# Weight splits three blocks ahead with four buffers; one pair for a slot's transposed rows, one buffer for the next stage's blocks

## The chip, the cores and the metric

The kernel runs on one core of a Trainium2 chip. Times are device microseconds (us) of one execution. The engines that matter are TensorE (PE for matmuls and transposes, PEld for loading its stationary operand), VectorE (DVE), ScalarE (ACT), GpSimd (POOL, which computes and also issues the indirect DMAs) and SyncE (SP, which issues the plain DMAs). Each engine works through its own queue in order.

## The reference

The kernel computes three layers on 1792 rows of 768 features, all in fp32:

```python
scores = scale * q @ k.T - log(S)
attn_out = sigmoid(scores) @ v                  # 4 x 12 heads, S = 448, 64 features
x = attn_out as [1792, 768]
expert_idx = argmax(x @ w_gate); gate_w = softmax(x @ w_gate)[expert_idx]
x = gate_w * (relu(x @ w1[expert_idx]) @ w2[expert_idx])      # 8 experts, 768 -> 1024 -> 768
g = x @ w2_gate;  out = (silu(g) * (x @ w2_val)) @ w2_out     # 768 -> 1536 -> 768
```

## The kernel before

Four stages follow one another: attention with the choice of experts, the expert stage, and two stages for the last layer, here called the first and the second GEMM.

The expert stage handles the 1792 rows in blocks of up to 128 rows of one expert, called slots. Slots 0 to 13 are the main ones, done one after the other; five half-filled ones (numbered from `NFX` = 17) run as background work between them. A matmul of fp32 quality is made of three with fp32r operands, so each weight block is split into a high part `whi` (a cast on ACT, line 811) and a low part `wlo` (a subtraction on DVE, line 813; for the first two blocks of w1 the last 256 columns are subtracted on POOL, line 815). `split_w` does that into the pool `wh`, which has `LA + 1` buffers for each part, and then has SP load the block of the next slot, if its expert differs (lines 817 to 820). `product` multiplies one block: six matmuls.

`seq` (line 844) is the list of blocks in their order: entries 0 to 3 are (1, 0, 4) to (1, 0, 7), the second half of w2 for slot 0; entries 4 to 9 are (0, 1, 0) to (0, 1, 5), w1 for slot 1; entries 10 to 15 are (0, 2, 0) to (0, 2, 5), w1 for slot 2; then w2 for slot 1, w1 for slot 3 and so on, 14 entries for each slot. The loop at line 1049 takes entry after entry: first `split_w` of the entry `LA` ahead, then all functions registered for this entry with `when`, in the order in which they were registered, then `product`. The whole is written inside `tc.manual_schedule()`: every engine issues its instructions in the order in which the program emits them. Across engines the framework inserts waits: an instruction that writes a tile waits until all uses of the tile that had the buffer before are over, wherever in the program these uses stand.

What is registered around the change:

- `gather(s)` (line 760): POOL issues an indirect DMA that fetches the rows of slot s into a tile `xg`. There are two buffers of `xg`. Slots 1 and 2 are gathered before entry 0; slot 3 by `early_x` of slot 1; the first background slot at entry 5.
- `early_x` (line 856) for slots 1 and 2: `transposes` puts the rows on PE through PSUM tiles `pt` (two buffers, shared by all transposes) into `xh` and `xl` (ACT casts, DVE subtracts). For slot 1 that is at entry 0, for slot 2 at entry 3. For later slots `tx` transposes at (1, s-2, 1) and evacuates at (1, s-2, 3).
- `bg_x`, `bg_h` (lines 926 and 961): six or four transposes of a background slot, at an entry whose kind and block number stand in `FREE`. For the first background slot `bg_x` comes at entry 10.
- `load_item` and `prep_next` (lines 668 and 892): load a block of the last layer's gate and value weights into a tile `w` (`WB` buffers) and split it into `wgh` and `wgl` (four buffers each). The first four are prepared during the expert stage, the others during the first GEMM (lines 1140, 1141 and 1150).

In the first GEMM, `gemm1(f, ci)` does 36 matmuls on up to 512 columns; its two halves use the gate block and the value block of f.

Of the kernel before, what the change touches and what calls it, by code (L numbers as in the profile page):

```python
# [22 lines left out]
def sigmoid_attention_moe_swiglu_kernel(  # L23
# [23 lines left out]
    KD = DM // P  # L47
# [26 lines left out]
    def split(hi, lo, src, eng=None):  # L74
        if eng is nc.vector:
            nc.vector.tensor_copy(hi, src)
        else:
            nc.scalar.copy(hi, src)  # L78
        nc.vector.tensor_sub(lo, src, hi.bitcast(F32))  # L79
# [60 lines left out]
    def load_w(kind, j, e, cond=None):  # L140
        src = (w1, w2)[kind][bass.ds(e, 1), j * P:(j + 1) * P, :].rearrange("o p f -> p (o f)")
        if cond is None:
            nc.sync.dma_start(raws[kind][j], src)
        else:
            nc.sync.dma_start(raws[kind][j], src, cond=cond)
# [500 lines left out]
            V.tensor_scalar(pos2, pos[:, hs_], 1, None, op0=ALU.logical_shift_left)  # L646
            V.tensor_tensor(pos2, pos2, upper.to_broadcast([P, NH0]), op=ALU.bitwise_or)

    LA = 2
    ectx = ExitStack()  # L650
    early = ectx.enter_context(tc.tile_pool(name="early", bufs=2, side="right", reuse_waits="tile"))
    ps_t = ctx.enter_context(tc.tile_pool(name="pst", bufs=2, space=PS, reuse_waits="tile"))
# [2 lines left out]
    mctx = ExitStack()  # L655
    wh = mctx.enter_context(tc.tile_pool(name="wh", bufs=LA + 1, reuse_waits="tile"))
    xp = mctx.enter_context(tc.tile_pool(name="xp", bufs=2, reuse_waits="tile"))
# [3 lines left out]
    KEEP = 2  # L661
    KS = K2 - KEEP

    WB = 2
    r64 = {}
    wsp = {}

    def load_item(key):
        kind, f = key
        r64[key] = early.tile([P, DM], F32, tag="w", name="w", bufs=WB)  # L670
        nc.sync.dma_start(r64[key], wgd["gv".index(kind) * K2 + f])

    def prep(key):
        hi = early.tile([P, DM], F32R, tag="wgh", name="wgh", bufs=4)
        lo = early.tile([P, DM], F32R, tag="wgl", name="wgl", bufs=4)
        split(hi, lo, r64.pop(key))
        wsp[key] = (hi, lo)
# [75 lines left out]
    xg = {}  # L753
    act = {}
# [5 lines left out]
    def gather(s):  # L760
        xg[s] = xp.tile([P, DM], F32, tag="xg", name="xg", bufs=2)
        nc.gpsimd.indirect_dma_start(
            out=xg[s][:, :], out_offset=None, in_=xd[:, :],
            in_offset=bass.IndirectOffsetOnAxis(ap=perm_g[:, s:s + 1], axis=0))

    def transposes(src, m, tag, bufs):
        hi = xp.tile([P, m * P], F32R, tag=tag + "h", name=tag + "h", bufs=bufs)
        lo = xp.tile([P, m * P], F32R, tag=tag + "l", name=tag + "l", bufs=bufs)
        pts = []
        for j0 in range(0, m, 4):  # L770
            mm = min(4, m - j0)
            pt = ps_t.tile([P, 512], F32, tag="tr", name="pt")
            for j in range(mm):
                nc.tensor.transpose(pt[:, j * P:(j + 1) * P],
                                    src[:, (j0 + j) * P:(j0 + j + 1) * P], ident)
            pts.append((pt, slice(j0 * P, (j0 + mm) * P), mm * P))

        def evac():
            for pt, sl, mm in pts:
                split(hi[:, sl], lo[:, sl], pt[:, :mm])  # L780
        return (hi, lo), evac

    def relu(s):
        hsb[s] = hsp.tile([P, FF], F32, tag="hs", name="hsb", bufs=1)
        nc.scalar.activation(hsb[s].rearrange("p (m f) -> p m f", m=2), hps.pop(s), AF.Relu)
# [3 lines left out]
    def yout(s):  # L789
        ysbs[s] = xp.tile([P, 2, HW + 1], F32, tag="ysb", name="ysb", bufs=1)  # L790
        nc.scalar.activation(ysbs[s][:, :, :HW], yps.pop(s)[:, :, :HW], AF.Copy,
                             scale=gsl[:, s:s + 1])

    def ystore_rows(s):
        ysb = ysbs.pop(s)
        nc.gpsimd.tensor_copy(ysb[:, :, HW:].bitcast(I32),
                              perm_g[:, None, s:s + 1].to_broadcast([P, 2, 1]))
        nc.gpsimd.indirect_dma_start(
            out=yd.rearrange("n h c -> n (h c)"),
            out_offset=bass.IndirectOffsetOnAxis(ap=pos[:, s:s + 1], axis=0),  # L800
            in_=ysb.rearrange("p h c -> p (h c)"), in_offset=None)
# [4 lines left out]
    def split_w(kind, s, j):  # L806
        w = (FF, DM)[kind]
        hi = wh.tile([P, FF], F32R, tag="hi", name="whi")
        lo = wh.tile([P, FF], F32R, tag="lo", name="wlo")
        r = raws[kind][j]  # L810
        nc.scalar.copy(hi[:, :w], r)  # L811
        w0 = w - PSH.get((kind, j), 0)
        nc.vector.tensor_sub(lo[:, :w0], r[:, :w0], hi[:, :w0].bitcast(F32))  # L813
        if w0 < w:
            nc.gpsimd.tensor_sub(lo[:, w0:w], r[:, w0:w], hi[:, w0:w].bitcast(F32))  # L815
        ws[kind, s, j] = (hi, lo)
        if s + 1 < NS0:
            if (s + 1) not in ev:
                load_ev(s + 1)
            load_w(kind, j, ev[s + 1], cond=nv[s + 1])  # L820
# [18 lines left out]
    EJ = 5  # L839
    YD, GJ = 3, 4  # L840
    PJ = (6, 4)
    XJ = (4, 7)
    NJ = 4
    seq = [(1, 0, j) for j in range(NJ, KF)] + [(0, 1, j) for j in range(KD)]
    for s in range(2, NS0 + 1):
# [6 lines left out]
    def when(kind, s, j, f):  # L852
        at.setdefault((kind, s, j), []).append(f)

    for s in (1, 2):
        def early_x(s=s):
            act[s], e = transposes(xg.pop(s), KD, "x", 2)
            e()
            if s == 1:
                gather(3)  # L860

        when(1, 0, XJ[s - 1], early_x)
    when(0, 1, 1, lambda: yout(0))
    when(0, 1, 2, lambda: ystore_rows(0))
    for s in range(1, NS0):
        e = {}

        def tx(s=s, e=e):
            act[s], e["x"] = transposes(xg.pop(s), KD, "x", 2)

        def th(s=s, e=e):
            hact[s], e["h"] = transposes(hsb.pop(s), KF, "h", 1)

        if s >= 3:
            when(1, s - 2, 1, tx)
            when(1, s - 2, 3, lambda e=e: e["x"]())
        if s == 1:
            when(0, 2, 1, lambda: relu(1))
        else:
            when(1, s - 1, 1, lambda s=s: relu(s))  # L880
        if s < L:
            when(0, s + 1, 3, th)
            when(0, s + 1, 4, lambda e=e: e["h"]())
        if s < L:
            when(*((0, s + 2, 1) if s + 2 <= L else (1, L, 0)), lambda s=s: yout(s))
            when(1, s + 1, YD, lambda s=s: ystore_rows(s))
        if s >= 4:
            when(1, s - 3, GJ, lambda s=s: gather(s))

    items = [(kind, f) for f in range(K2) for kind in "gv"]  # L890

    def prep_next(key):
        prep(key)
        i = items.index(key) + WB
        if i < len(items):
            load_item(items[i])

    pre = [lambda i=i: load_item(items[i]) for i in range(WB)]
    pre += [lambda key=key: prep_next(key) for key in items[:4]]
    for i, f in enumerate(pre):  # L900
        when(1, 3 + i, PJ[i % 2], f)
    R0 = E
    when(0, R0 + 2, 0, lambda: (make_yT(0), load_y(0)))
    for j in range(KD):
# [95 lines left out]
    def extra():  # L1000
        for s in [*range(NS0, NFX), *range(NFX + NH0, NS)]:
            ev[s] = nc.values_load(slot_e[0:1, s:s + 1], engines=[SP], min_val=0, max_val=E - 1,
                                   skip_runtime_bounds_check_because=why)
            sq = [(kind, s, j) for kind, m in ((0, KD), (1, KF)) for j in range(m)]
            for kind, _, j in sq:
                load_w(kind, j, ev[s])
            gather(s)
            act[s], e = transposes(xg.pop(s), KD, "x", 2)
            e()
            for key in sq[:LA]:  # L1010
                split_w(*key)
            for i, key in enumerate(sq):
                if i + LA < len(sq):
                    split_w(*sq[i + LA])
                if key == (1, s, 0):
                    relu(s)
                    hact[s], e = transposes(hsb.pop(s), KF, "h", 1)
                    e()
                product(*key)
            yout(s)  # L1020
            ystore_rows(s)

    hbp = post = ymid = None
    with tc.manual_schedule():
# [16 lines left out]
        yps[0] = ps_a.tile([P, 2, 512], F32, tag="a", name="yps")  # L1041
        for idx in range(LA):
            split_w(*seq[idx])
# [5 lines left out]
        for idx, key in enumerate(seq):  # L1049
            if idx + LA < len(seq):  # L1050
                split_w(*seq[idx + LA])
# [17 lines left out]
        with tc.If(nsl > NS0):  # L1069
            extra()  # L1070
# [68 lines left out]
        e = gemm1(0, 3)  # L1139
# [6 lines left out]
        for f in range(2, K2):  # L1146
            for ci in range(NC):
                e = gemm1(f, ci)
# [95 lines left out]
```

## Time and profile before

| | us |
|---|---|
| median of 3 runs | 1111.11 (1110.35 to 1111.57) |
| the profiled execution | 1114.54 |
| span of its instructions | 1112.7 |
| PE busy | 1071.4 (96% of the span) |
| DVE busy | 554.2 (50%) |
| ACT busy | 468.2 (42%) |
| POOL busy | 273.1 (25%) |

The span runs from the first to the last instruction of the profiled execution; 1.84 us of that execution lie around it. The expert stage takes from about 225 us to 581 us of the span, the first GEMM to about 928 us, the second to about 1097 us. "Granted clock" is TensorE's clock as a share of full speed (2.4 GHz); 0.5 is the lower level of 1.2 GHz.

In the timeline a row begins with its start and the time that it covers, both in us, then engine, line, operation, and output <- inputs; "xN" are N instructions of the kind in one row; brackets hold the idle time of the engine just before and what ended it. Matmuls overlap in the pipeline, so the distance between starts tells what one costs, not its length. In the windows view a row begins with the stretch and its length, then come the busy us (and instructions) of PE, PEld, DVE, ACT and POOL, the mean granted clock, the busy share of the DMA engines and GB/s.

### The profile page before, as it was taken

What the parts mean: (1) busy time and instruction counts of PE and PEld (TensorE: products, weight loads), DVE (VectorE), ACT (ScalarE), POOL (GpSimd) and SP (SyncE); (2) the same over time, 40 slices, a digit from 0 to 9 for tenths busy, and PEclk for the clock granted to TensorE, in tenths of its full rate; (3) what the DMA queues carried; (4) which work ended last, traced back from release to release, by engine and by line L of the source; (5) the groups of instructions that cost most, each with busy time, mean ns of one, the idle gap of its engine ahead of it and who ended that gap; (6) DMA issues with size and microseconds to landing.
All of it is one profiled execution on the core that took longest, in us unless ns stands there. A gap on an engine that the chain in (4) does not pass through costs nothing. (4 is left out here: it accounts for less than half of the span.)

```text
span 1112.7 us, 16190 instructions
## 1 busy us (share of the span) xinstructions
PE 1071.4 (96%) x5970; PEld 850.2 (76%) x5970; DVE 554.2 (50%) x851; ACT 468.2 (42%) x646; POOL 273.1 (25%) x234
## 2 busy tenths in 40 slices
PE   8999999899999999888989999999999999999996
PEld 5556555476767677766778888888888889999996
DVE  4686777676665677666643334444432225111110
ACT  6676766166566677566642211111111124112110
POOL 3656566341132222121110022222210000000101
PEclk9999999899999999999999999999999999999999
DMA  9999996845585776868441334444321134322220
GB/s 206 272 278 253 271 252 202 321 143 183 194 288 163 267 236 201 289 220 279 137 153 57 118 124 147 147 147 147 118 77 51 68 100 131 102 76 76 80 86 29
DMA packets 130533, 186.06 MB, mean 167 GB/s; under 512 B 51520, under 2 KB 95040, under 8 KB 130448
## 3 DMA queue, kind: packets, MB, share of 16 engines
q1 hardware_dynamic: 124400, 156.04, 45.3%
q0 software_dynamic: 6048, 28.92, 7.4%
q8 instruction: 49, 0.80, 0.3%
q14 instruction: 36, 0.29, 0.1%
HBM read 195.99 MB, written 40.85 MB: 213 GB/s over the span
## 5 line engine op out<-in xcount | busy, mean ns | idle before, releaser
L734 PE MATMUL psf<-y,wgh 128*128 128x512 f32 (+1 forms) x1152 | 321.0, 365 | 0.0
L813 DVE TENSOR_TENSOR wlo<-wraw,whi 128x768 fp32r<-128x768 f32 (+1 forms) x186 | 196.9, 1074 | 115.8 <-ACT whi L811 113.2
L734 PEld LDWEIGHTS psf<-y,wgh 128*128 128x128 f32 x1152 | 206.3, 189 | 32.8
L811 ACT CAST whi<-wraw 128x768 fp32r<-128x768 f32 (+1 forms) x186 | 170.3, 925 | 119.1 <-PE yps L835 59.9
L734 PE MATMUL psf<-y,wgl 128*128 128x512 f32 (+1 forms) x576 | 209.5, 364 | 0.0
L1185 PE MATMUL po<-y,hh 128*128 128x384 f32 x672 | 145.5, 334 | 0.6 <-ACT ob L1189 0.6
L739 ACT ACTIVATE sg<-psf 128x512 f32<-128x512 f32 (+1 forms) x48 | 26.1, 544 | 244.7 <-PE psf L734 244.7
L734 PEld LDWEIGHTS psf<-y,wgl 128*128 128x128 f32 x576 | 109.0, 189 | 17.2
L740 DVE TENSOR_TENSOR sg<-psf,sg 128x512 f32<-128x512 f32 (+1 forms) x48 | 30.0, 625 | 183.4 <-ACT sg L739 183.3
L1185 PEld LDWEIGHTS po<-y,hh 128*128 128x128 f32 x672 | 119.0, 188 | 0.9 <-ACT ob L1189 0.9
L236 ACT ACTIVATE a<-sc,logs 112x896 f32<-112x896 f32 x96 | 91.9, 1016 | 58.0 <-PE sc L234 58.0
L1185 PE MATMUL po<-y,hl 128*128 128x384 f32 x336 | 87.3, 334 | 0.0
L79 DVE TENSOR_TENSOR hl<-ht,hh 128x1280 fp32r<-128x1280 f32 x14 | 20.9, 1492 | 123.8 <-ACT hh L78 123.8
L1209 POOL DMA_INDIRECT out_dram<-ob,perm_c x13 | 13.0, 998 | 264.2 <-ACT ob L1208 264.2
L245 PE MATMUL pu<-a,vraw 112*64 112x448 f32 x384 | 77.5, 545 | 0.0
L173 POOL TENSOR_SCALAR w<-w 128x768 f32<-128x768 f32 x24 | 55.6, 2317 | 60.3 <-ACT w L162 60.2
L815 POOL TENSOR_TENSOR wlo<-wraw,whi 128x256 fp32r<-128x256 f32 x26 | 35.8, 1387 | 138.3 <-ACT whi L811 131.5
L78 ACT CAST hh<-ht 128x1280 fp32r<-128x1280 f32 x14 | 17.7, 1266 | 118.7 <-PE po L1185 118.7
L173 POOL TENSOR_SCALAR hl<-hl 128x768 f32<-128x768 f32 x12 | 27.5, 2292 | 138.1 <-ACT hl L162 138.1
L1185 PEld LDWEIGHTS po<-y,hl 128*128 128x128 f32 x336 | 60.9, 188 | 0.0
L835 PE MATMUL yps<-whi,hh 128*128 128x384 f32 x216 | 59.2, 355 | 0.0
L245 PEld LDWEIGHTS pu<-a,vraw 112*64 112x64 f32 x384 | 25.5, 136 | 40.9 <-issue 40.8
(235 smaller groups left out, 1600.7 us busy)
## 6 DMA issues: line engine op xcount, KB each, us to landing
wraw<-in_moe_w_dram SPq DMA_DIRECT2D x108, 384.0 KB
wraw<-in_moe_w_dram SPq DMA_DIRECT2D x78, 512.0 KB
ring<-in_moe_w_dram SPq DMA_DIRECT2D x30, 512.0 KB
ring<-in_moe_w_dram SPq DMA_DIRECT2D x40, 384.0 KB
r<-in_moe_w_gate_dram SPq DMA_DIRECT2D x12, 768.0 KB
wgd<-w POOLq DMA_DIRECT2D x24, 384.0 KB, 6.5
r<-in_moe_w_val_dram SPq DMA_DIRECT2D x12, 768.0 KB
w<-wgd SPq DMA_DIRECT2D x24, 384.0 KB
```

The costliest lines, as they stand in the source:

```text
L79: nc.vector.tensor_sub(lo, src, hi.bitcast(F32))
L173: nc.gpsimd.tensor_scalar(w, w, TINY, None, op0=ALU.is_ge)
L236: nc.scalar.activation(am[i][:, c], sc[:CP, :, :S], AF.Sigmoid, bias=logs[:CP], scale=SCALE)
L245: nc.tensor.matmul(pu[h * D:(h + 1) * D, :S], vt[:, h, c], a[:, c, h], start=(c == 0), stop=(c == C - 1))
L734: nc.tensor.matmul(ps[:, i, :cn], st[:, a], mv[:, j, :cn], start=(j == 0 and m == 0), stop=(j == KD - 1 and m == 2))
L739: nc.scalar.activation(sg[:, :cn], ps[:, 0, :cn], AF.Sigmoid)
L740: nc.vector.tensor_mul(sg[:, :cn], ps[:, 0, :cn], sg[:, :cn])
L811: nc.scalar.copy(hi[:, :w], r)
L813: nc.vector.tensor_sub(lo[:, :w0], r[:, :w0], hi[:, :w0].bitcast(F32))
L815: nc.gpsimd.tensor_sub(lo[:, w0:w], r[:, w0:w], hi[:, w0:w].bitcast(F32))
L835: nc.tensor.matmul(ps[:, m, :w], st[:, a], mv[:, m * w:(m + 1) * w], start=(j == 0 and i == 0), stop=(j == m_ - 1 and i == 2))
L1185: nc.tensor.matmul(po[:, m, :HW], st[:, f], wo[f][mv][:, m * HW:(m + 1) * HW], start=(f == 0 and x == 0), stop=(f == K2 - 1 and x == 2))
```

## The change

The weight split looks three entries ahead instead of two, and `wh` therefore has four buffers. The tiles `xh`, `xl` of a slot's transposed rows have one buffer each instead of two, and the tiles `w` of the last layer's blocks one instead of two. `early_x` of slot 2 moves from entry 3, (1, 0, 7), to entry 10, (0, 2, 0), where it is registered ahead of the first `bg_x`. The first `load_item` and the four early `prep_next` move by some entries; the second early `load_item` is gone, since `prep_next` loads the next block.

```diff
-    LA = 2
+    LA = 3
...
-    WB = 2
+    WB = 1
...
-    XJ = (4, 7)
...
     for s in (1, 2):
         def early_x(s=s):
-            act[s], e = transposes(xg.pop(s), KD, "x", 2)
+            act[s], e = transposes(xg.pop(s), KD, "x", 1)
             e()
             if s == 1:
                 gather(3)
 
-        when(1, 0, XJ[s - 1], early_x)
+        when(*((1, 0, 4) if s == 1 else (0, 2, 0)), early_x)
...
         def tx(s=s, e=e):
-            act[s], e["x"] = transposes(xg.pop(s), KD, "x", 2)
+            act[s], e["x"] = transposes(xg.pop(s), KD, "x", 1)
...
-    pre = [lambda i=i: load_item(items[i]) for i in range(WB)]
+    pre = [lambda: load_item(items[0])]
     pre += [lambda key=key: prep_next(key) for key in items[:4]]
     for i, f in enumerate(pre):
-        when(1, 3 + i, PJ[i % 2], f)
+        when(1, 4 + i, PJ[i % 2], f)
```

The same count of one buffer is put into `extra()`, which runs only when there are more slots than the 14 main and five background ones.

## Rows read from the trace of the kernel before

**Rows 1.** Busy time of each engine in the expert stage (windows view).

```profile
225.00:581.00 356.00, 334.18 (x1711) 253.62 (x1709) 236.69 (x272) 231.36 (x304) 84.07 (x88) 0.99 0.63 212
```

**Rows 2.** What PE waited for, 225 to 582 us: total, times, longest (waits).

```profile
PE pt L934 <- issue: 5.3, 3, 2.6
PE pt L964 <- DVE xl L79: 5.2, 2, 2.6
PE pt L964 <- DVE hl L79: 5.2, 2, 2.6
...
PE yps L835 <- DVE wlo L813: 0.7, 3, 0.2
```

**Rows 3.** The same view for PEld, the same stretch.

```profile
PEld yps L835 <- DVE wlo L813: 1.9, 4, 0.6
...
PEld hps L835 <- POOL wlo L815: 1.3, 4, 0.4
```

**Rows 4.** One background transpose that waits, all engines (timeline, 339 to 343 us).

```profile
339.58 0.83 ACT L811 CAST whi<-wraw 128x768 fp32r<-128x768 f32 x1 [0.21 <-PE yps L835]
340.32 0.85 ACT L78 CAST xh<-pt 128x512 fp32r<-128x512 f32 x2
341.32 1.01 DVE L79 TENSOR_TENSOR xl<-pt,xh 128x512 fp32r<-128x512 f32 x2
342.15 0.63 PE L964 MATMUL pt<-ident,bhs 128*128 128x128 f32 x4 [2.61 <-DVE xl L79]
```

**Rows 5.** A product that waits for its low part (timeline of PE, 265 to 267 us).

```profile
265.59 0.51 PE L835 MATMUL yps<-whi,hl 128*128 128x384 f32 x2
265.94 0.51 PE L835 MATMUL yps<-whi,hh 128*128 128x384 f32 x2
266.70 0.62 PE L835 MATMUL yps<-wlo,hh 128*128 128x384 f32 x2 [0.25 <-DVE wlo L813]
```

**Rows 6.** Transposes of slot 1 and of the first background slot (timeline of PE).

```profile
231.28 0.82 PE L774 MATMUL pt<-ident,xg 128*128 128x128 f32 x6
...
245.06 0.82 PE L934 MATMUL pt<-ident,xg 128*128 128x128 f32 x6
```

**Rows 7.** POOL in the same stretch: gathers of slots 3, 17 and 4 (timeline).

```profile
232.37 0.95 POOL L762 DMA_INDIRECT xg<-xd,perm_g  x1 [8.40 <-PE pt L774]
...
238.47 0.97 POOL L762 DMA_INDIRECT xg<-xd,perm_g  x1
...
243.68 2.92 POOL L815 TENSOR_TENSOR wlo<-wraw,whi 128x256 fp32r<-128x256 f32 x2 [1.59 <-ACT whi L811]
246.76 1.81 POOL L762 DMA_INDIRECT xg<-xd,perm_g  x1 [0.16 <-issue]
```

**Rows 8.** Issue to landing: gather at 232.37, at 246.76, all 16 after 225 us.

```profile
DMA to landing us min/median/max: 3.7/3.7/3.7
...
DMA to landing us min/median/max: 7.2/7.2/7.2
...
DMA to landing us min/median/max: 3.7/5.6/8.5
```

**Rows 9.** DMA traffic and granted clock in three stretches (windows view).

```profile
245.00:249.00 4.00, 4.00 (x22) 3.38 (x21) 2.92 (x3) 2.71 (x3) 3.41 (x3) 1.00 0.81 307
...
342.90:346.20 3.30, 3.30 (x14) 2.86 (x12) 0.96 (x1) 1.32 (x2) 0.00 (x0) 0.53 0.01 2
...
528.40:531.80 3.40, 3.37 (x21) 3.40 (x22) 1.00 (x2) 1.65 (x3) 0.00 (x0) 1.00 0.00 0
```

**Rows 10.** First GEMM: loads of `w` on SP, traffic after one, a value half (timeline, windows).

```profile
634.89 2.49 SPq L671 DMA_DIRECT2D w<-wgd  x2
...
643.55 0.62 PE L734 MATMUL psf<-y,wgh 128*128 128x512 f32 x2
...
650.77 8.48 SPq L671 DMA_DIRECT2D w<-wgd  x2
...
653.60:656.50 2.90, 2.90 (x15) 2.39 (x14) 0.00 (x0) 0.51 (x2) 0.00 (x0) 1.00 0.00 0
```

More of the change, by code (lines that the diff above doesn't have):

```diff
@@ L1007, in extra @@
             gather(s)
-            act[s], e = transposes(xg.pop(s), KD, "x", 2)
+            act[s], e = transposes(xg.pop(s), KD, "x", 1)
             e()
```

## The prediction

> **What bounds the kernel now.** I read the page's engine shares first, then the windows by stage, then the waits of PE and PEld in the stage that the change touches, then the timeline around each kind of wait. In the expert stage PE is busy 334.2 of 356.0 us, while DVE and ACT are busy about two thirds [rows 1]. So PE is the bound, and whatever holds it there goes into the total at full price: in the first GEMM PE has no idle time left that could absorb it (2.90 of 2.90 us in the stretch shown [rows 10]). What holds PE? Its named waits before transposes of background slots make up most of the list: 5.3, 5.2 and 5.2 us, at most 2.6 us each [rows 2]. Waits for a weight's low part are small: 0.7 us on PE in three places [rows 2], 1.9 and 1.3 us on PEld [rows 3], which partly cover the same time.
>
> **Three ahead with four buffers.** This can only remove waits for weight parts. The clearest place: pairs of matmuls of w2 start 0.35 us apart, and one pair starts 0.76 us after the pair before it, idle for `wlo` [rows 5]; that costs 0.41 us. Three such places are in the list [rows 2], so about 1.2 us; the shorter waits on PEld [rows 3] I put at about 0.6 us, since a wait of PEld is partly covered by the matmul that runs. One entry more of lead is worth three pairs of 0.35 us or more, about 1 us, against waits of at most 0.6 us [rows 3], so I take all of them as gone: -1.8 us. The bounds are 0 (what is late next is the same DVE queue) and -3.9 us (the three sums 0.7, 1.9 and 1.3 added as if none overlapped).
>
> The larger waits, those of the background transposes, stay. In the one shown, PE has finished a product, ACT casts a weight block, then the slot's rows, DVE subtracts, and only then is a PSUM tile free [rows 4]. The cast ahead of the rows was itself released by the product just finished. With three buffers, the split two ahead takes the buffer of the preceding entry; with four buffers, the split three ahead takes the buffer of that same entry. The chain keeps its length, 2.6 us.
>
> The split runs one entry earlier throughout, and the load behind it on SP with it, so a block still has 14 entries between its load and its split. One cast more ahead of entry 0 lies beside the fp32 products that run on PE until the transposes at 231.28 [rows 6]. Cost of both: nothing.
>
> **One pair for the transposed rows.** From slot 3 on, rows are evacuated at (1, s-2, 3), when the products of slot s-1 that read the single pair are three entries past. The writer finds it free; no wait. For slot 2 this isn't so at entry 3, and that is why its `early_x` has to stand behind entry 9.
>
> **Slot 2's rows at entry 10.** The step consists of six transposes on PE, two casts, two subtracts, and no DMA. Moved as work they cost what they cost now. But the step is moved past something on POOL's queue: the gather of the first background slot, emitted at entry 5. There are two `xg` buffers. At entry 5 one holds slot 3, the other slot 2, which is now read only at entry 10. So POOL's gather waits for PE's transposes at entry 10, and right behind these, at the same entry, stand the transposes of that very background slot, which need the gathered rows. PE works in order: it waits for a whole DMA that is under way today while PE works (issued at 238.47 [rows 7], used at 245.06 [rows 6]).
>
> How long? The place is 245.06 us. Slot 2's transposes no longer run at entry 3, so PE gets there about 0.6 us earlier and spends that again: they end near 245.3. A gather released by transposes starts about 0.3 us after their end (231.28 + 0.82, then 232.37 [rows 6, 7]), so at 245.6. It lands 3.7 to 8.5 us after issue, median 5.6 [rows 8]. Which? The gather at 246.76 is the nearest in place and takes 7.2 us [rows 7, 8]; the loads of the background weights are under way then, at 307 GB/s [rows 9], and they will be in the changed kernel too, as SP reaches them before the blocked work. I take 7.2: landing at 252.8, 7.7 us later than the background transposes start today. Bounds: 3.7 gives +4.2 us, 8.5 gives +9.0 us.
>
> A page says less: the Trainium skill, "DMA: Bandwidth & Descriptors", section "Anatomy of one DMA — SWDGE (gpsimd) path", fits such a transfer as 2.0 us plus its bytes at 436 GB/s, 2.9 us for 384 KB, an estimate of that page. By it this term would be +3.4 us; the trace disagrees, its fastest gather took 3.7 us [rows 8].
>
> Queued behind the waiting gather on POOL are a store of output rows (a short copy and an indirect DMA of about 1 us) and the low parts of (0, 2, 0) and (0, 2, 1), about 1.5 us each [rows 7]. The first is ready near 250, the second near 251.5, both before PE resumes at 252.8; if the gather lands at its fastest, the first is just in time. SP's loads for slot 3 wait for these two parts, some 6 us longer than now, and are wanted eleven entries later, over 15 us. ACT's evacuation of slot 2's rows ends within the wait. None of these adds to it.
>
> **The clock.** After one 2.6 us wait the clock that PE was granted had a mean of 0.53 over 3.30 us, which is the lower level of 1.2 GHz nearly throughout, and cost 3.30 x 0.47 = 1.5 us; after another of the same length, before 528.4, it stayed at 1.00 [rows 9]. A wait of 7.5 us will hardly go by without a fall, though part of the slow time may lie in the wait. I take +1.5 us, bounds 0 and +3.1 (two such stretches). The later 2.6 us waits will fall differently too; I count that as zero on the mean and up to two stretches either way.
>
> **One buffer for `w`.** The Trainium skill, "Trainium Kernel Development and Optimization", section "Best Practices", advises double buffers to overlap DMA with compute; by that rule the first GEMM would now wait for loads. In the trace, a load issued at 650.77 moves nothing more after 653.6, 2.8 us later [rows 10]. The tightest place is the pair prepared back to back: the second load would be issued at 634.89, land near 637.7, be split in about 1.8 us, and is first wanted at 643.55 [rows 10]: 4 us to spare. Elsewhere a whole `gemm1` lies between. Cost: nothing. The earlier `prep_next` of the expert stage are a slot or more apart, and SP's queue loses one early load.
>
> **Sum.** 7.7 + 1.5 - 1.8 = +7.4 us. The profiled execution took 1114.54 us with a span of 1112.7; it would be 1120.1 in span and about 1121.9. The median of the runs is 3.4 us below that execution, so 1111.1 + 7.4 = 1118.5 us.
>
> **Rivals.**
> A, the gather is not the last to arrive. If the rows are there in time (the framework finds a place for them after all), PE still waits at entry 10 for the PSUM tiles that slot 2's rows occupy: 2.6 us by the chain of rows 4. Then 2.6 - 1.8 = +0.8, 1111.9 us. Against it: two buffers can't hold three live tiles.
> B, faster: the extra buffer lets the cast in the chain of rows 4 run before PE's product ends. 0.83 us would fall out of each of the seven background waits [rows 2], 5.8 us; with the 1.8 that is 7.6. It decides only if the gather takes its shortest time and the clock holds: 4.2 - 7.6 = -3.4, 1107.7 us. Against it: the buffer arithmetic above.
> C, the lead doesn't do what it says: weight waits stay, since DVE's queue and not the buffer sets them. 7.7 + 1.5 = +9.2, 1120.3 us.
> D, the rule on double buffers holds in the first GEMM: `w` lands later than the 4 us to spare allow; with a load as slow as the slowest gather, 8.5 us instead of 2.8 [rows 8, 10], 1.7 us more, 1120.2 us.
>
> **How the numbers follow.** Forecast 0.72, A 0.11, B 0.04, C 0.10, D 0.03. The forecast's own bounds run from 4.2 - 3.9 = +0.3 to 9.0 + 3.1 = +12.1, with both ends unlikely as sums of extremes. A range from 1111.8 to 1122.3 takes in A, C and D and leaves out B and the high end. A measurement tells apart about 0.2% here, 2.2 us. Faster by more: B and a trace of luck with the clock, 0.05. Within 0.2% (1108.9 to 1113.3): A and the forecast's low end, 0.15. Slower: 0.80.
>
> **What would show it.** After: one new wait of PE of about 7 us before `bg_x`'s first transposes (near 245 us), ended by the gather; POOL idle until then, released by the transposes at line 774; weight waits on PE gone; the background waits still at 2.6 us; the first GEMM without idle time. The prediction is wrong if that gather is issued before slot 2's rows are transposed, or if the background waits shrink.

## The result, and the profile after

| | us |
|---|---|
| median of 5 runs after | 1120.31 (1118.38 to 1121.70) |
| median of 5 runs of before beside them | 1111.11 (1109.74 to 1113.92) |
| ratio after / before | 1.0078, 95% interval 1.0058 to 1.0099 |
| the profiled execution after, its span | 1118.38, 1116.5 |
| PE, DVE, ACT, POOL busy | 1070.0, 554.2, 467.6, 275.5 |

The changed kernel is 0.8% slower. PE does as much work as before (1071.4 us then); the difference is waiting and clock. From line 842 on, lines stand one earlier than before (934 is now 933, 964 is 963); the others kept their numbers.

What PE waited for in the expert stage of after, 225 to 586 us (waits view: engine, output, line, releaser, then total us, times, longest). It answers [rows 2].

```profile
PE pt L933 <- DMA xg<-xd,perm_g: 6.7, 1, 6.7
PE pt L933 <- issue: 5.3, 3, 2.6
PE pt L963 <- DVE xl L79: 5.2, 2, 2.6
PE pt L963 <- DVE hl L79: 5.2, 2, 2.6
```

One line is new, the wait for gathered rows. The three below it are the old ones to the tenth. They hold seven waits of background transposes, of which five take 2.6 us; the other two, both under "issue", take 1.2 and 1.5 us (at 314.6 and 376.8 us). No line for `wlo` is left, here or on PEld, where [rows 2, 3] had 0.7, 1.9 and 1.3 us.

The place of the new wait, PE of after (timeline; it answers the second row of [rows 6]):

```profile
250.23 1.51 PE L933 MATMUL pt<-ident,xg 128*128 128x128 f32 x6 [6.74 <-DMA xg<-xd,perm_g]
251.40 1.20 PE L835 MATMUL hps<-whi,xh 128*128 128x512 f32 x2
```

And POOL's queue in the same stretch of after (timeline; it answers [rows 7]), with the gather's landing below (view of line 762, 243 to 244.5 us; it answers [rows 8]):

```profile
232.69 2.92 POOL L815 TENSOR_TENSOR wlo<-wraw,whi 128x256 fp32r<-128x256 f32 x2 [1.00 <-ACT whi L811]
243.77 0.97 POOL L762 DMA_INDIRECT xg<-xd,perm_g  x1 [8.16 <-PE pt L774]
244.75 0.48 POOL L796 COPY ysb<-perm_g 128x2 int32<-128x2 int32 x1
245.52 1.00 POOL L798 DMA_INDIRECT yd<-ysb,pos  x1 [0.29 <-POOL ysb L796]
246.54 1.41 POOL L815 TENSOR_TENSOR wlo<-wraw,whi 128x256 fp32r<-128x256 f32 x2
...
DMA to landing us min/median/max: 6.3/6.3/6.3
```

The gather of the first background slot went out at 238.47 in before. Now POOL stands idle for 8.16 us until PE's transposes of slot 2 (line 774) have read the second `xg`, and only then issues it. PE, which has just done these transposes, stands idle for the whole transfer. The two places hold one another up: POOL waits for PE's entry 10, then PE's entry 10 waits for POOL.

Behind the wait the clock is low. Windows of after (stretch and length, then busy us of PE, PEld, DVE, ACT, POOL, granted clock, DMA share, GB/s); the last row is the stretch that answers the low one of [rows 9]:

```profile
247.60:251.00 3.40, 0.77 (x4) 0.80 (x5) 0.00 (x0) 0.00 (x0) 0.35 (x1) 0.56 0.73 299
251.00:254.40 3.40, 3.40 (x11) 2.82 (x10) 0.00 (x0) 0.01 (x1) 1.00 (x1) 0.50 0.24 36
...
346.60:350.00 3.40, 1.59 (x11) 1.62 (x12) 1.91 (x4) 0.83 (x3) 0.00 (x0) 1.00 0.00 0
```

From 251.0 to 254.4 PE works at 1.2 GHz throughout: 3.40 x 0.50 = 1.7 us lost. With what is lost on either side of it (the six transposes at 250.23 take 1.17 us up to the next matmul, 0.57 in before) the fall costs about 2.2 us. In the other direction, the fall that before had near 343 us isn't there in after.

Where did the span's 3.8 us (1112.7 to 1116.5) come from? I set the starts of the same matmuls side by side, before against after. At the start of the stage after is 1.6 us early (the end of attention, which the change doesn't touch). From entry 4 to entry 10 it loses 8.1 us, of which 0.7 are slot 2's transposes, gained at entry 3, and 0.6 are the clock under the background transposes; from entry 10 to the first w2 block of slot 1 it loses 1.6 us more (clock). Then it wins 2.4 us in eight small steps of 0.53 us or less (weight waits) and 1.1 us at the missing fall of the clock. The first GEMM, from the start of its first matmul to that of its last, takes 365.7 us in after, 365.8 in before. The medians differ by 9.2 us, more than the two profiled spans: the profiled execution of before was 3.4 us above its median, that of after the fastest of its five. The runs themselves differ by clock: the two of after at a granted clock of 0.990 over the whole run took 1118.4 and 1118.6 us, the three at 0.985 to 0.987 took 1120.3 to 1121.7.

### The profile page after: what moved, and what is told of

Same layout as the page of the kernel before. It is cut to its first block, busy times and chain, and to the rows that moved or that the text cites. A ratio compares the mean times of both kernels' runs of the same rounds, so it can differ in the third digit from the quotient of the medians.

```text
span 1116.5 us, 16190 instructions
## 1 busy us (share of the span) xinstructions
PE 1070.0 (96%) x5970; PEld 850.9 (76%) x5970; DVE 554.2 (50%) x851; ACT 467.6 (42%) x646; POOL 275.5 (25%) x234
```

## The experiments

Each ran on one chip together with the kernel before, and its ratio is to those runs. My theory was that of the prediction: the held gather is the loss, three entries of lead win about 2 us, the single `w` costs nothing. The rivals were its A to D.

**The move alone.** The kernel before, with only slot 2's rows moved to entry 10.

```diff
-        when(1, 0, XJ[s - 1], early_x)
+        when(*((1, 0, 4) if s == 1 else (0, 2, 0)), early_x)
```

> The kernel before with one edit: early_x of slot 2 at entry 10 instead of entry 3; the split stays two ahead, all buffer counts as before. Theory (the gather of the first background slot is held by the two xg buffers until slot 2's rows are transposed): one new wait of PE of 6 to 8 us at line 934 near 245 us, 1111.1 + 7 to 9 = 1118 to 1120 us. Rival (the loss comes from splitting three ahead or from the smaller buffer counts): no new wait, 1111 us.

1122.25 us, ratio 1.0088 (1.0067 to 1.0110). PE in its trace (timeline):

```profile
252.38 1.51 PE L934 MATMUL pt<-ident,xg 128*128 128x128 f32 x6 [6.92 <-DMA xg<-xd,perm_g]
```

This one edit costs as much as the whole change. What the other edits bring is not seen beside it.

**All but the lead.** The kernel after, two entries ahead (`LA = 2`, three buffers).

> The changed kernel with the split two ahead (three buffers), the rest of the change kept. Theory: the long wait stays, and 1.8 us of weight waits come back: 1122 us against 1120.3 for the change. Rival (a longer lead brings nothing because the subtractions on DVE are the limit): the same as the change, 1120.3 us. Rival (the lead itself costs): faster than the change.

1121.37 us, ratio 1.0075 (1.0050 to 1.0100), as for the whole change: by the ratios the lead is worth nothing here. The gather's wait is 6.8 us and the span 1120.1 us, 3.6 more than after's, of which 1.4 us stand ahead of the expert stage. The starts of the same matmuls, side by side, give the lead 2.6 us in weight waits. The intervals can't tell this from nothing.

**A third `xg`.** The same, two entries ahead, with three buffers for `xg`, so that the gather doesn't wait.

```diff
-        xg[s] = xp.tile([P, DM], F32, tag="xg", name="xg", bufs=2)
+        xg[s] = xp.tile([P, DM], F32, tag="xg", name="xg", bufs=3)
```

> The changed kernel with the split two ahead and three xg buffers instead of two. Theory: the gather is issued near 238 us again, and at entry 10 PE waits only for the PSUM tiles of slot 2's rows, 2 to 2.6 us: about 1113.7 us with the weight waits that two ahead leaves. Rival (the step at entry 10 is slow by itself, whatever the gather does): the 7 us stay, 1120 us or more.

1118.62 us, ratio 1.0061 (1.0036 to 1.0085). The gather goes out at 237.3 again and its wait is gone. What is late next at entry 10 (timeline of PE in this kernel):

```profile
246.74 1.54 PE L933 MATMUL pt<-ident,xg 128*128 128x128 f32 x6 [2.38 <-DVE xl L79]
```

This is rival A's wait, for the PSUM tiles of slot 2's rows: 2.4 us where A put 2.6. The span fell by 5.3 us, to 1114.8, the median by only 2.8, and the time is 4.9 us above the 1113.7 that I expected. The rival is out as to its wait, since the 7 us are gone; with the two intervals overlapping, this run alone didn't settle how much the held gather costs.

**The held gather taken away from the kernel after.** The first background slot's rows go into an idle tile of another group, and everything else is as in after, three ahead among it.

```diff
-        xg[s] = xp.tile([P, DM], F32, tag="xg", name="xg", bufs=2)
+        if s == NFX:
+            xg[s] = early.tile([P, DM], F32, tag="yt", name="xg", bufs=4)
+        else:
+            xg[s] = xp.tile([P, DM], F32, tag="xg", name="xg", bufs=2)
```

> The kernel after, all of it, but the first background slot's rows are gathered into a tile of the `yt` group, which is idle until the rows of the final stage are read back, so that no third `xg` tile is wanted at once. Theory (the loss is the held gather and what it brings): the gather goes out at about 237 us again, the PE wait for DMA xg (6.7 us) goes, and entry 10 waits 2.4 us for a PSUM tile as in two_ahead_three_xg, here with the weight waits (2.4 us in sum) gone as well: 1118.6 - 2.4 = 1116.2 us; if the low clock behind the wait goes too, down to 1112 (rival A of the prediction, 1111.9). Rival (three blocks ahead are worth nothing once the gather is early, rival C): as two_ahead_three_xg, 1118.6 us. Rival (the hold was not the cause): as after, 1120.3 us.

1114.35 us beside 1114.98 of before, ratio 0.9999 (0.9987 to 1.0010). Its POOL issues the gather early, and PE's longest list entry of after is replaced (timeline of POOL, waits of PE; lines from 761 on stand three later than in after):

```profile
237.40 1.77 POOL L765 DMA_INDIRECT xg<-xd,perm_g  x1 [0.15 <-DMA wraw<-in_moe_w_dram]
```

```profile
PE pt L936 <- issue: 5.3, 3, 2.6
PE pt L966 <- DVE hl L79: 5.2, 2, 2.6
PE pt L966 <- DVE xl L79: 5.2, 2, 2.6
PE pt L936 <- DVE xl L79: 2.4, 1, 2.4
```

One tile's place accounts for the whole loss: 1.0078 becomes 0.9999, and the intervals are far apart. What is left is rival A's sum, a wait of 2.4 us against the weight waits, with a result of nothing; behind that wait too the clock is low for a while, from 247.7 us. Against the run with the third `xg` this kernel has one entry more of lead and no wait for `wlo`, and the ratio falls from 1.0061 to 0.9999. That isn't a clean price for the lead: the two ran on different chips, the tile differs too, and the spans of the two traces are only 1.9 us apart (1114.8 and 1112.9). In the starts of the same matmuls the weight waits are again 2.6 us (0.2%); the rest of the 0.6% I can't place.

**Background work five entries later**, in the kernel after, so that the gather would have time.

```diff
             while (seq[b0 + d][0], seq[b0 + d][2]) not in FREE:
                 d += 1
+            if k == 0 and d == 0:
+                d = 5
```

> The changed kernel with the first background slot's transposes five entries later, at (0, 2, 5); split three ahead, two xg buffers. Theory: the gather is still issued only behind slot 2's transposes, but it lands while PE does five products of 1.4 us each; PE waits 0 to 1 us there: 1111.1 - 1.8 = 1109.3 us, up to 1110.5. Rival (the lead of three is worth nothing): 1111.1 us. Rival (the loss is elsewhere than in that wait): 1118 us or more.

1118.98 us, ratio 1.0051 (1.0029 to 1.0072): ten us above what I expected. PE's waits behind slot 2's transposes in its trace (timeline):

```profile
243.14 0.73 PE L835 MATMUL hps<-whi,xh 128*128 128x512 f32 x2 [0.96 <-ACT xh L78]
...
246.01 0.80 PE L835 MATMUL hps<-wlo,xh 128*128 128x512 f32 x1 [1.91 <-POOL wlo L815]
...
257.24 0.94 PE L933 MATMUL pt<-ident,xg 128*128 128x128 f32 x5 [1.19 <-issue]
...
261.09 1.94 PE L952 MATMUL bps<-ring,xbt 128*64 128x512 f32 x8 [1.41 <-ACT xbt L969]
```

The gather is still held back on POOL, and behind it on that queue stand the store and the low parts of (0, 2, 0) and (0, 2, 1). In after these finished within PE's wait for the rows; with that wait moved, they are the next to be late, at 1.91 us. ACT's evacuation of slot 2's rows, at 0.96 us, comes out the same way, and PE's first background products then wait 1.4 us for their rows. Some 5.5 us of waits, and a low clock from 245.0 to 251.8 us (granted clock 0.50), eat the gain: the first w2 block of slot 1 starts as long after entry 0 as in after. Moving the reader alone doesn't help while the queue is held; the spare tile, which frees the queue and leaves the reader where it is, wins the whole loss back.

**The lead alone.** The kernel after with slot 2's rows back at entry 3 and two pairs for them; to make room, the ring of background weights has three buffers instead of four.

```diff
-    RB = 4
+    RB = 3
```

> The changed kernel with slot 2's rows transposed at entry 3 again and two pairs for transposed rows; to make room, three ring buffers for the background weights instead of four. Split three ahead, one buffer for w. Theory: the gather is issued near 238 us, no wait at entry 10, weight waits gone: 1111.1 - 1.8 = 1109.3 us. Rival (the lead is worth nothing): 1111.1 us. If three ring buffers are too few, a wait of PE for the ring shows by name.

1126.26 us, ratio 1.0127 (1.0103 to 1.0152), 17 us above what I expected. What PE waited for in it, first line of the list (waits):

```profile
PE bps L952 <- DMA ring<-in_moe_w_dram: 8.2, 5, 3.2
```

The buffer that I gave up was needed, so this is no price of the lead. It shows that of the small buffers in this kernel the ring's fourth is not one to take.

**The single `w` alone.** The kernel before with `WB = 1` and the change's places for the first loads.

> The kernel before with one buffer for w and the first loads and splits of these blocks placed as in the change; all else as before. Theory: 1111.1 us, no wait of PE for a split of w in the first GEMM. Rival (double buffering is needed there): waits of PE for wgh or wgl, from 1 us in one place up to 1 us for each of 20 blocks, 1112 to 1131 us.

1115.53 us beside 1114.02, ratio 1.0027 (1.0007 to 1.0048). In its trace (of the fastest of ten runs, span 1108.3) PE has no wait for `wgh` or `wgl`, and the first GEMM takes 365.6 us. So the traced mechanism of rival D is not there. The 0.27% goes with the clock: the mean granted clock of its ten runs is 0.9892, that of the runs of before beside them 0.9916, which is 0.24% of the time. Why it was lower in them, no run shows.

**The order within an entry.** The background waits are the larger item, and the prediction left them alone. In the kernel before, the functions of an entry now come ahead of the split for a later entry.

```diff
-            if idx + LA < len(seq):
-                split_w(*seq[idx + LA])
             for f in at.get(key, ()):
                 f()
+            if idx + LA < len(seq):
+                split_w(*seq[idx + LA])
```

> The kernel before with one edit: in the loop the registered functions run ahead of the weight split instead of behind it, so an evacuation stands ahead of the weight cast on ACT and DVE. Theory (the cast is part of the chain that a background transpose waits for): the waits of 2.6 us fall to about 1.8 us, 5.8 us less in seven places, while weight waits grow, as two ahead leaves no room: 1105 to 1111 us. Rival (the cast runs beside that chain): waits stay at 2.6 us, 1111 us or more.

1098.11 us, ratio 0.9868 (0.9840 to 0.9895), below the 1105 to 1111 us that I expected. Its background waits (waits of PE, 220 to 590 us; compare [rows 2]), and the place that answers [rows 4] (timeline):

```profile
PE pt L964 <- DVE xl L79: 3.1, 2, 1.6
...
PE pt L934 <- issue: 1.5, 1, 1.5
PE pt L964 <- DVE hl L79: 1.4, 2, 0.7
```

```profile
336.05 0.85 ACT L78 CAST xh<-pt 128x512 fp32r<-128x512 f32 x2
336.18 0.96 DVE L813 TENSOR_TENSOR wlo<-wraw,whi 128x768 fp32r<-128x768 f32 x1 [0.16 <-ACT whi L811]
336.79 0.84 ACT L811 CAST whi<-wraw 128x768 fp32r<-128x768 f32 x1
337.05 1.01 DVE L79 TENSOR_TENSOR xl<-pt,xh 128x512 fp32r<-128x512 f32 x2
337.88 0.63 PE L964 MATMUL pt<-ident,bhs 128*128 128x128 f32 x4 [1.57 <-DVE xl L79]
```

Before, DVE had this row ahead of the same `xl` (timeline of the kernel before, the stretch of [rows 4]):

```profile
339.40 2.00 DVE L813 TENSOR_TENSOR wlo<-wraw,whi 128x768 fp32r<-128x768 f32 x2 [0.74 <-ACT whi L811]
```

Now the rows' casts run ahead of the entry's own weight cast, and of DVE's two weight subtractions one is left in front. The wait is 1.57 us instead of 2.61. Over the stage the three named groups fall from 15.7 to 6.0 us: two of the seven waits are gone, and the others take 0.7 to 1.6 us. Three smaller groups of waits of before (`bps` for `xbt` 1.4 us, `pt` for `xbt` 0.6 and for `y` 0.6) have no line any more. That is 12.3 us, and the ratio is worth 14.7 (1114.02 x 0.0132). The low-clock stretches that before has from 343.1, 462.5 and 582.0 us aren't in this trace (it has one from 225.9 that before hasn't), and its span is 17.3 us shorter. But that part isn't shown to follow from the shorter waits: the trace of the single `w` has the background waits of before and no fall near the first two places either.

**The same order with other parts.** The kernel after with this order:

> The kernel after with the functions registered for an entry ahead of split_w; the gather stays held by the third `xg`. Theory (the gather's wait and the background waits are separate prices): the wait for DMA xg stays at 6.4 to 7 us with its low clock (2 us), the background waits fall from 18.4 to about 6 us, and the time is 1096 + 6.7 + 2 = 1104.7 us. Rival (with the evacuations earlier the `xg` tile comes free earlier too, or the wait is hidden): 1098 us, no PE wait for DMA xg above 2 us.

1103.17 us, ratio 0.9894 (0.9876 to 0.9911); its wait for the gather is 5.6 us, somewhat less than the 6.4 to 7 expected, and the low clock behind it stays:

```profile
251.36 1.51 PE L933 MATMUL pt<-ident,xg 128*128 128x128 f32 x6 [5.59 <-DMA xg<-xd,perm_g]
```

The held gather and the background waits are two separate prices: the held gather makes 0.8% under the old order (1.0078 against 0.9999) and 0.7% under the new one (0.9894 against 0.9824, the spare tile with this order, below). The kernel of the lead alone, ring of three among it, with this order:

> The kernel of lead_alone with the registered functions ahead of the weight split. Theory: both gains add up, as three ahead leaves room for the later cast: 1111.1 - 1.8 - 5.8 = 1103.5 us. Rival (the cast is off that chain): 1109.3 us. Rival (weights become late even with three ahead): waits of PE for wlo of more than 2 us in total, above 1106 us.

1104.80 us, ratio 0.9909 (0.9879 to 0.9939); the ring's waits are still 6.0 us in three places, and the order brings its 2% here as well.

The spare tile with this order, which no longer holds the gather and keeps three ahead:

> spare_tile with the functions registered for an entry ahead of split_w of the block three entries ahead. evac_first (two ahead, functions first) took 1098.1 us. Theory (three ahead is worth its 1.8 to 2.4 us of weight waits wherever nothing else comes last): 1096 us, PE's waits for wlo gone, background waits about 6 us in sum as in evac_first. Rival (early_x(2) three entries later costs more than that, by a PSUM tile that isn't free at entry 10 or by a low clock behind it): 1099 to 1101 us.

1095.16 us, ratio 0.9824 (0.9807 to 0.9841), the fastest of all kernels here. Its largest waits (PE, 225 to 586 us):

```profile
PE pt L966 <- DVE xl L79: 3.1, 2, 1.6
PE pt L936 <- issue: 1.5, 1, 1.5
...
PE pt L936 <- DVE xl L79: 1.4, 1, 1.4
```

Entry 10 waits 1.4 us, and behind it the clock stays at full speed. And the same two ahead:

> spare_tile_evac_first with the weight split two entries ahead instead of three (and so three buffers), nothing else. Theory (three ahead is worth the weight waits it removes, here 1.6 + 0.4 + 0.3 us on PEld as in evac_first, and nothing else): the waits for wlo come back and the time is 1095.2 + 2 = 1097 us, ratio to before about 0.984. Rival (the third block of lead also keeps the casts and subtractions out of the way of the rows' evacuation, so more hangs on it): background waits above the 6.6 us of spare_tile_evac_first by another 2 us or more, 1099 us or more, ratio 0.986. Rival (worth nothing): 1095.2 us, ratio 0.982.

1097.45 us, ratio 0.9860 (0.9841 to 0.9878). PEld's waits for `wlo` come back, 2.3 us in sum (waits of PEld); the background waits are 7.2 us in sum against 6.6:

```profile
PEld hps L838 <- POOL wlo L818: 1.8, 5, 0.4
PEld yps L838 <- DVE wlo L816: 0.3, 1, 0.3
PEld hps L838 <- DVE wlo L816: 0.2, 1, 0.2
```

The medians differ by 2.3 us, but the two ran on different chips; the ratios differ by 0.36%, 4.0 us, and their intervals just touch. Of that, 0.24% stand in the granted clock (mean 0.9952 with three ahead, 0.9928 with two). In the starts of the same matmuls, over the expert stage, three ahead is worth 2.1 us: 1.4 in weight waits and the rest before background transposes. So where little else is late it is worth about the waits that it removes; whether it also brings the higher clock isn't shown.

## Why the prediction was right, point by point

**The held gather** was the step that decided, and it held: two `xg` buffers and three live tiles. Where it put the gather's issue behind slot 2's transposes, POOL's row shows just that. The size came out a little smaller: 6.3 us to landing against 7.2, and 6.8 us net against 7.7. (8.1 us from entry 4 to entry 10, less 0.7 for the moved transposes and 0.6 of low clock.) Taking the nearest gather was no better a choice than the median of all: 7.2 is 0.9 us too long, 5.6 would have been 0.7 too short. Nor was its traffic a good guide, since the DMA engines moved 298 GB/s in all while that gather of 7.2 us was under way, and 364 during this shorter one. By the fit of the Trainium skill, "DMA: Bandwidth & Descriptors", section "Anatomy of one DMA — SWDGE (gpsimd) path", 2.9 us as an estimate, the term would have been less than half of the forecast; the trace disagrees with 6.3 us.

**The clock** was taken too low: 2.2 us instead of 1.5. The step took one 3.3 us stretch as the price; the stretch is twice as long, part of it within the wait. The later falls came out 1.1 us in after's favour, within the bounds.

**Three ahead** removed every weight wait: 2.4 us in the trace against 1.8. Rival C is out as a mechanism: in after and in the spare-tile kernel no wait for `wlo` is left, and the starts of matmuls give the lead 1.4 to 2.6 us in every pair of traces. The ratios alone don't show it, since those with and without the lead are the same beside the held gather.

**The background waits unchanged**: right, all seven are as before. Rival B is out. The prediction speaks of 2.6 us throughout; only five of the seven are that long, which changes none of its terms. The three that [rows 2] has under "issue" (timeline of PE in before):

```profile
307.82 1.05 PE L934 MATMUL pt<-ident,xg 128*128 128x128 f32 x6 [1.21 <-issue]
...
371.89 0.84 PE L934 MATMUL pt<-ident,xg 128*128 128x128 f32 x6 [1.52 <-issue]
...
498.21 0.84 PE L934 MATMUL pt<-ident,xg 128*128 128x128 f32 x6 [2.56 <-issue]
```

But the step named only the cast on ACT as what stands ahead of the rows. DVE's two subtractions stand there too, which rows 4 didn't show, and the order of an entry's emission sets both. That was 1.3%, outside this change, that the prediction walked past.

**The work queued behind the gather on POOL**: right in after, where it ends within PE's wait, at 247.95 us. The low parts were put at 1.5 us each and took 0.7 there (two in 1.41 us, row at 246.54). The later background start shows how little slack that was: the low parts were 1.9 us late at once.

**One `w`**: the first GEMM is unchanged, so rival D is out. The Trainium skill's advice in "Trainium Kernel Development and Optimization", section "Best Practices", to double-buffer, isn't borne out for `w` (365.6 us with one buffer alone against 365.8). Elsewhere in this kernel a buffer did matter: the fourth of the ring, and a third place for gathered rows.

**Rival A** is the kernel with the spare tile: +0.8 us forecast, -0.1 measured by the ratio (0.1% either way).

**The sum.** Put together, the three terms measured 6.8 + 2.2 - 2.4 = +6.6 us against +7.4. Their errors (-0.9, +0.7 and -0.6 us) are small, and partly cancel by luck. The runs' ratio makes it +8.7 us (1111.11 x 0.0078). The forecast of 1118.5 us lies 1.8 us below the median and within the range; about 2 us of the difference stand in no term. The granted clock of the runs can hold them: the profiled run of after has 0.990, the median one 0.987, 0.3% less.

## What to carry to other kernels

When a step is moved later, list what it still holds (buffers above all) and who on another in-order queue needs that next: here six transposes moved by seven entries held one tile, and that cost 0.8%. Before giving an engine more lead, look at the order in which each entry's work is emitted: what PE waits for next should stand ahead of what is wanted three entries later, and that order was worth 1.3 to 2.2% in the kernels tried here, the tile's place 0.8%. When a wait is taken away, read the queue behind it: the later background start changed 6.7 us of one wait into four smaller ones.

## What the runs showed that I had not expected

- After a wait of nearly the same length the low clock lasted differently: about 6.8 us in after (wait 6.7 us), about 10.2 us in the move alone and in the kernel of two ahead (waits 6.9 and 6.8 us). The span of these two is 1120.1, after's 1116.5.
- The same waits came with different clocks: the trace of before has low stretches near 343, 462 and 582 us, that of the single `w`, with the same background waits, only one near 577 us, and its span is 4.4 us shorter. A few microseconds between two traces can be clock alone.
- One indirect gather of the same 384 KB took 3.7 us from issue to landing at 232 us in before, while the DMA engines moved 106 GB/s in all, and 6.3 us at 244 us in after, at 364 GB/s in all.
